# Attention beside a 2-D spectral filter on one core: spent query space reused for exp buffers, longer batches of key steps, and a closing product in three rounded parts

## The chip, the core and the metric

The kernel runs on one core of a Trainium2 chip. The metric is the device time of one execution in microseconds. The kernel before took 642.26 us as the median of three runs (642.26 to 642.81). The engines named below are PE (TensorE; PEld is its loading of weights), DVE (VectorE), ACT (ScalarE), POOL (GpSimd) and SP (SyncE, which here only starts DMAs).

## The reference

Two independent halves, put side by side in the output (2048 x 896):

```python
# half A: B=1, S=2048, D=448, H=16 heads of Dh=28, one key and one value head for all
q = (x @ wq).reshape(B, S, H, Dh).transpose(0, 2, 1, 3)
k, v = x @ wk, x @ wv
p = softmax(einsum("bhqd,bkd->bhqk", q, k) * Dh ** -0.5)
a = einsum("bhqk,bkd->bhqd", p, v).transpose(0, 2, 1, 3).reshape(B, S, H * Dh) @ wo
# half B: x of 2048 x 448, weights of 2048 x 225
y = irfft2(rfft2(x) * (w_r + 1j * w_i))
```

Everything is float32. Where a float32 matmul would be slow, the kernel splits an operand into a rounded high part and a low rest (F32R) and adds the three larger of the four products.

## The kernel before, in words

**The stages.** First come the projections of half A and the first transform of half B. They leave the queries of all heads in `qraw` (128 partitions x 4 groups x 2048 positions, on chip, 1 MB for each quarter of 512 positions), the split keys in `ka` and the values with a column of ones in `vs`. Then follows the main loop, which is nearly the whole time: attention for 4 quarters `c` of the queries times 4 groups `g` of four heads times 16 blocks `kc` of 128 keys, 256 *steps* in that order. A step has, for each of its four heads, a *score* matmul (line 872: 128 keys x 512 queries into one bank of PSUM), an exp of scale times score on ACT into an exp buffer on chip (line 816), and a product with the values (line 827, `flush`), which adds up over the 16 steps in one bank `po`. An exp buffer `p` holds two heads; there are `P_BUFS = 8` of them, so four steps.

**Batches.** Steps are taken in batches, listed in `PLAN`: all scores of a batch are issued first, then the products. `spread` writes out a batch of `n` steps as a string in order of issue: "-" is a score whose exp ACT does straight from PSUM, "k" a score of the batch's last step, which DVE copies to a `k` tile in SBUF (line 878) so that its bank is free early; its exp is done later, in place, two heads in one instruction of ACT (line 895), and the products of this *kept* step come in the next batch (`kept`). "e" is a kept score that ACT exps straight from PSUM. Letters for other work stand among the scores: "A" and "B" are the two matmul units of half B's middle stage (`fft2_a`, `fft2_b`, lines 561 to 563), "Z" its last stage (`fft3_a`, line 660, and `fft3_b`, line 674), "W" a quarter of an output projection of half A (`wo_unit`, line 736), "X" four W, "Y" two Z. `start` and `rest` shift the places. In the list before there are 50 batches: two of one step, four of two, 18 of five and 26 of six.

**What sets the order.** PE, DVE and ACT run in the order of the program. Eight banks of PSUM serve scores, units and the running sum; `take` picks the one that a running estimate (`clock`) has free first and `give` returns it after its last reader. `exps` issues an exp only while fewer than eight buffers are held. DVE's other work (splits of queries in `build_q`, division and split of results in `norm`, splits of weights) waits in `queue` and is put between by `passed` where the estimate has DVE free; `need` forces it. `after(step)` starts what hangs on a step: loads of the next stage (`later`), and at `step % 16 == 3` the split of the next group's queries from `qraw` into `qa`, which eight small DMAs and a large one on SP then spread.

**The end.** After the last batch (lines 907 to 940) the sum of the last group is transposed and divided in four blocks; for each block of 128 queries nine rounded products of the first three groups (`partial`) and one float32 product of the last group with `w3` (`final`, line 918) make the output, which ACT copies (line 741) and sends from its own DMA queue (line 746). A branch follows that is taken only when scores could overflow; it reads `qraw` and isn't taken here.

Of the kernel before, what the change touches and what calls it, by code (L numbers as in the profile page):

```python
# [10 lines left out]
F32 = mybir.dt.float32  # L11
# [12 lines left out]
NG = 4  # L24
NC = 4
# [22 lines left out]
PLAN += [spread(5, "BA", 4, 0.9, 0.6)] + [spread(5, "A")] + 6 * [spread(5, "BA", 4, 0.9, 0.6)]  # L48
PLAN += [spread(5, "BA", 4, 0.75, 0.6)] + 3 * [spread(5, "BA", 4, 0.9, 0.6)] + 2 * [spread(6, "X")]
PLAN += [spread(5, "BA", 4, 0.9, 0.6)] + [spread(6, "BAX")] + [spread(5, "BAB", 4, 0.9, 0.6)]  # L50
PLAN += [spread(6, "BX")] + [spread(6, "Y")] + [spread(5, "")] + 2 * [spread(6, "Y")]
PLAN += [spread(6, "Y", 4, 0.9, 0.6)] + [spread(6, "X")] + [spread(6, "X", 4, 0.9, 0.6)] + [spread(6, "X")]
PLAN += [spread(6, "Y")] + [spread(6, "X", 4, 0.9, 0.6)] + 3 * [spread(6, "Y")]
PLAN += [spread(6, "Y", 4, 0.9, 0.73)] + [spread(6, "Y")] + [spread(6, "Y", 4, 0.9, 0.73)]
PLAN += 3 * [spread(6, "X")] + [spread(6, "Y")] + [spread(6, "X", 4, 0.9, 0.73)] + [spread(5, "Y")]
PLAN += [spread(6, "Y")] + [spread(6, "Y", 4, 1.2)] + [spread(5, "Y")]


WARM = 10, 10
# [3 lines left out]
def kernel(ctx: ExitStack, tc: tile.TileContext, t: dict):  # L63
# [462 lines left out]
    def need(key):  # L526
        while key not in done:
            pop()
# [8 lines left out]
    def at_once(work=640, engine="dve"):  # L537
        clock[engine] = max(clock[engine], clock["pe"] + 200) + work
# [196 lines left out]
                    continue  # L735
                mm(p, x[c][:, g, s], w, start=(g == 0 and n == 0), stop=(g == NG - 1 and n == 2))  # L736

    def wo_out(p, c, k, on_act=False):
        y = pp.tile([128, D], F32, name="yb", tag="p") if on_act else ap.tile([128, D], F32, name="ya")
        if on_act:  # L740
            nc.scalar.activation(y, p, AF.Copy)
        else:
            nc.vector.tensor_copy(y, p)
            at_once()
        r0 = c * CW + k * 128
        (nc.scalar if on_act else nc.sync).dma_start(t["oa"][r0:r0 + 128], y)

    wps = {}

# [17 lines left out]
    def at(step, f, *a):  # L767
        later.setdefault(max(step, 0), []).append((f, a))
# [35 lines left out]
    order = [(c, g) for c in range(NC) for g in range(NG)]  # L804
    kept, po = [], {}

    waiting, held, count = deque(), [0], {}

    def exps():

        while waiting and (waiting[0][2] % 2 or held[0] < P_BUFS):
            sc, tiles, h = waiting.popleft()
            if h % 2 == 0:
                tiles.append(pp.tile([128, 2, CW], F32, name="p"))
                held[0] += 1
            nc.scalar.activation(tiles[-1][:, h % 2], sc, AF.Exp, scale=SCALE)  # L816
            at_once(477, "act")
            give(sc, "act")

    def flush(first, rest=()):  # L820

        for c, g, kc, ps, normal in (*first, *rest):
            n = count[c, g] = count.get((c, g), 0) + 1
            if n == 1:
                po[c, g] = take()
            for i in range(4):
                mm(po[c, g][32 * i:32 * i + 32], vs[:, kc], ps[i // 2][:, i % 2], start=(n == 1), stop=(n == 16))  # L827
            passed(864)
            if n == 16:
                o = osb[c, g] = ap.tile([128, CW], F32, name="osb")  # L830
                nc.vector.transpose(o, po[c, g])  # L831
                at_once()
                if (c, g) != order[-1]:
                    give(po[c, g])
                    norms.append((c, g))
            if normal:
                held[0] -= 2
# [12 lines left out]

    begin = 0
    for tokens in PLAN:
        n = sum(k in "-ke" for k in tokens) // 4
        steps = [(*order[(begin + i) // 16], (begin + i) % 16) for i in range(n)]
        for i in range(n):
            if (begin + i) // 16:
                need(("q", (begin + i) // 16))
        new, lazy, x = [], [], {"-": 0, "k": 0}
        keep = [pp.tile([128, 2, CW], F32, name="k", bufs=4) for _ in range(2)]
        for k in tokens:  # L860
            if k not in "-ke":
                f, *a = todo[k].popleft()
                f(*a)
                continue
            kind = "-" if k == "-" else "k"
            i, h = divmod(x[kind], 4)
            x[kind] += 1
            if kind == "-" and h == 0:
                new.append([])
            c, g, kc = steps[i if kind == "-" else n - 1]  # L870
            sc = take()
            begun.append(mm(sc, ka[:, kc * 128:(kc + 1) * 128], qa[c, g][:, h], start=True, stop=True))  # L872
            passed(232)
            if kind == "-":
                waiting.append((sc, new[i], h))
                exps()
            elif k == "k":
                nc.vector.tensor_copy(keep[h // 2][:, h % 2], sc)  # L878
                at_once()
                give(sc)  # L880
                lazy.append(h)
            else:
                nc.scalar.activation(keep[h // 2][:, h % 2], sc, AF.Exp, scale=SCALE)
# [4 lines left out]
        steps = [(*s, ps, ps is not keep) for s, ps in zip(steps, [*new, keep])]  # L888
        passed(290)
        flush(steps[:1] + kept if n > 4 else kept + steps[:-1], steps[1:-1] if n > 4 else [])  # L890
        kept = steps[-1:]
        clock["act"] += 470 * len(lazy)
        if len(lazy) == 4:
            for p in keep:
                nc.scalar.activation(p, p, AF.Exp, scale=SCALE)  # L895
        else:
            for h in lazy:
                p = keep[h // 2][:, h % 2]
                nc.scalar.activation(p, p, AF.Exp, scale=SCALE)
        after(begin + n - 1)  # L900
        begin += n
    while norms:
# [2 lines left out]
        pop()  # L905

    c = NC - 1
    w3 = ap.tile([128, D], F32, name="w3", tag="ya")
    nc.sync.dma_start(w3, t["wo"][:, NG - 1])
    ws = []  # L910

    def partial(k):
# [1 line left out]
        wo_mm(ws[k], c, k, range(NG - 1))  # L914

    def final(k):
        p = ws[k]
        mm(p, on[:, 128 * k:128 * k + 128], w3, start=False, stop=True)
        wo_out(p, c, k, True)


    flush(kept)
# [1 line left out]
    for k in range(4):  # L924
        divide(c, NG - 1, k)
        s = slice(128 * k, 128 * k + 128)
        nc.vector.transpose(on[:, s], osb[c, NG - 1][:, s])
    for k in (0, 1):
        partial(k)
    for k in (2, 3):  # L930
# [7 lines left out]
    a, b, d = spare  # L938
    rv = nc.values_load(bits.bitcast(I32)[0:1, 0:1])
    with tc.If(rv > int(np.float32(BOUND).view(np.int32))), tc.tile_pool(name="g1", bufs=1) as g1:  # L940
        kf = g1.tile([32, S], F32, name="kf")
        k4 = g1.tile([128, S], F32, name="k4")
        nc.vector.tensor_copy(kf, ka[0:32].bitcast(F32))
# [183 lines left out]
```

## Time and profile before

| | |
|---|---|
| median of 3 runs | 642.26 us (642.26 to 642.81) |
| profiled execution: its time, its span | 642.82 us, 641.0 us |
| granted PE clock | 1.0 |
| busy: PE, ACT, DVE, POOL | 635.7, 550.7, 372.3, 80.1 us |
| first score of the main loop | 70.45 us |
| first score of step 10 (batches of five begin) | 90.21 us |
| first score of step 109 | 304.58 us |
| last product with the values ends | 626.38 us |

How to read it: "busy" counts the time in which at least one instruction of the engine runs. A line in order of time gives the start, the length, the engine, the line of the program, the operation, output<-input, shapes, how many in a row, and in brackets how long the engine was idle before and what ended that. Matmuls overlap: the time that one takes of PE is the distance to the next one's start, not its own length. A float32 matmul stands as two records.

### The profile page before, as it was taken

How to read it: one execution, taken by the hardware profiler on the slowest of the kernel's cores; microseconds unless marked ns; L12 is line 12 of the kernel's file. 1: busy time of each engine (PE TensorE's matmuls, PEld its weight loads, DVE VectorE, ACT ScalarE, POOL GpSimd, SP SyncE). 2: the span in 40 equal slices, each digit the busy share in tenths (PEclk: the TensorE clock that was granted, in tenths of full speed). 3: DMA queues.
4: the chain of work that ended last, by engine and by line, in shares of the span. 5: the costliest groups of instructions: out<-in, count | busy, mean ns of one | idle time of the engine just before them, and what ended most of it. 6: DMA issues, size and time to landing. Idle time of an engine off the chain costs nothing.

```text
span 641.0 us, 12024 instructions
## 1 busy us (share of the span) xinstructions
PE 635.7 (99%) x4470; PEld 381.8 (60%) x4470; DVE 372.3 (58%) x683; ACT 550.7 (86%) x1011; POOL 80.1 (12%) x150
## 2 busy tenths in 40 slices
PE   9999999999999999999999999999999999999997
PEld 6877655556555556655655566556655566556555
DVE  5999628889997934766543523264545332264521
ACT  5554999999999998988899898998999898998981
POOL 3021401011311110000120300003031100200110
PEclk9999999999999999999999999999999999999999
DMA  8755971554835521214241403123241303140001
GB/s 271 268 161 159 262 175 47 143 126 111 205 102 128 142 59 49 79 47 136 63 103 44 115 16 85 39 57 92 55 120 43 88 15 81 44 127 2 30 31 60
DMA packets 36113, 63.83 MB, mean 100 GB/s; under 512 B 7905, under 2 KB 23922, under 8 KB 35084
## 3 DMA queue, kind: packets, MB, share of 16 engines
q1 hardware_dynamic: 30832, 49.60, 28.0%
q0 software_dynamic: 4640, 12.48, 7.8%
q10 hardware_dynamic: 576, 0.92, 0.4%
q8 instruction: 36, 0.59, 0.4%
q14 instruction: 29, 0.24, 0.1%
HBM read 30.04 MB, written 14.75 MB: 70 GB/s over the span
## 4 chain that ended last, share of the span: by engine, by line
PE 98%; DMA 1%; ACT 0%; SPq 0%; issue 0%; ACTq 0%
PE s L872 31%; PE s L827 22%; PE sx L827 9%; PE s L347 6%; PE po L872 5%; PE po L827 4%; PE s L736 4%; PE sx L872 4%; PE s L145 2%; PE s L674 2%; PE s L660 2%; PE pbb L164 1%; DMA raw<-wq 1%; PE s L562 1%; PE s L561 1%; PE s L563 1%
## 5 line engine op out<-in xcount | busy, mean ns | idle before, releaser
L816 ACT ACTIVATE p<-s 128x512 f32<-128x512 f32 x650 | 345.9, 631 | 33.4 <-PE s L872 27.5
L872 PE MATMUL s<-qa,ka 128*128 128x512 f32 x798 | 236.1, 405 | 0.0
L872 PEld LDWEIGHTS s<-qa,ka 128*128 128x128 f32 x798 | 146.7, 188 | 67.7 <-issue 26.8
L878 DVE COPY k<-s 128x512 f32<-128x512 f32 x129 | 82.5, 682 | 106.6 <-PE s L872 106.6
L827 PE MATMUL s<-p,vs 128*32 128x512 f32 x1024 | 121.7, 595 | 0.0
L895 ACT ACTIVATE k<-k 128x1024 f32<-128x1024 f32 x88 | 90.3, 1108 | 0.0
L827 PEld LDWEIGHTS s<-p,vs 128*32 128x32 f32 x1024 | 30.8, 109 | 67.6 <-issue 65.6
L816 ACT ACTIVATE p<-po 128x512 f32<-128x512 f32 x89 | 56.2, 631 | 9.2 <-PE po L872 8.5
L816 ACT ACTIVATE p<-sx 128x512 f32<-128x512 f32 x85 | 53.6, 630 | 3.1 <-PE sx L872 1.9
L827 PE MATMUL sx<-p,vs 128*32 128x512 f32 x416 | 49.3, 594 | 0.0
L872 PE MATMUL po<-qa,ka 128*128 128x512 f32 x120 | 49.2, 410 | 0.0
L872 PE MATMUL sx<-qa,ka 128*128 128x512 f32 x106 | 42.4, 400 | 0.0
L700 POOL DMA_DIRECT2D ol<-ol x36 | 18.1, 510 | 135.9 <-DVE ol L723 69.0
L827 PE MATMUL s<-k,vs 128*32 128x512 f32 x256 | 33.4, 594 | 0.0
L684 POOL TENSOR_TENSOR yo<-y 128x226 f32<-128x226 f32 x16 | 9.5, 596 | 188.0 <-DVE y L680 110.9
L872 PEld LDWEIGHTS po<-qa,ka 128*128 128x128 f32 x120 | 22.5, 188 | 14.6 <-issue 9.2
L827 PEld LDWEIGHTS sx<-p,vs 128*32 128x32 f32 x416 | 12.5, 110 | 27.9 <-issue 27.6
L831 DVE STREAM_TRANSPOSE osb<-s 128x512 f32<-128x512 f32 x10 | 7.2, 715 | 37.0 <-PE s L827 37.0
L878 DVE COPY k<-po 128x512 f32<-128x512 f32 x29 | 19.8, 681 | 14.3 <-PE po L872 14.3
L827 PE MATMUL po<-p,vs 128*32 128x512 f32 x208 | 25.0, 595 | 0.0
L872 PEld LDWEIGHTS sx<-qa,ka 128*128 128x128 f32 x106 | 19.9, 188 | 6.7 <-issue 2.5
L347 PE MATMUL s<-xh,wqh 128*128 128x512 f32 x56 | 23.0, 410 | 0.1
(217 smaller groups left out, 788.1 us busy)
## 6 DMA issues: line engine op xcount, KB each, us to landing
qa<-qa SPq DMA_DIRECT2D x15, 512.0 KB
raw<-xa SPq DMA_DIRECT2D x16, 256.0 KB
xb<-xb SPq DMA_DIRECT2D x8, 512.0 KB
qa<-qh SPq DMA_DIRECT2D x64, 64.0 KB
qa<-ql SPq DMA_DIRECT2D x60, 64.0 KB
ob<-yo SPq DMA_DIRECT2D x16, 226.0 KB
t<-bs SPq DMA_DIRECT2D x16, 225.0 KB
wr<-wr POOLq DMA_DIRECT2D x16, 225.0 KB, 4.2
```

The source lines that it names most:

```text
L145: mm(pa[r0:r0 + 32, e, o0:o0 + n], f[:, 2 * r + k, 2 * p + e, h], cs1[:, 2 * r + k, :n], start=True, stop=True)
L347: mm(pq, w[:, j, gs], x[:, j], start=(j == 0 and n == 0), stop=(j == 3 and n == 1))
L660: mm(pz[:w, j], c2["c", q][:, j, o0:o0 + w], c2["F", q][:, j], start=True, stop=True)
L674: mm(py[:, k], z[:w, r, js], cs3[:w, k], start=True, stop=True)
L684: nc.gpsimd.tensor_tensor(yo[:, 0:2], y1[:, 0], y1[:, 1], op=ALU.add)
L700: nc.gpsimd.dma_start(ol[c][o, g].bitcast(F32), ol[c][r, 0].bitcast(F32))
L736: mm(p, x[c][:, g, s], w, start=(g == 0 and n == 0), stop=(g == NG - 1 and n == 2))
L816: nc.scalar.activation(tiles[-1][:, h % 2], sc, AF.Exp, scale=SCALE)
L827: mm(po[c, g][32 * i:32 * i + 32], vs[:, kc], ps[i // 2][:, i % 2], start=(n == 1), stop=(n == 16))
L872: begun.append(mm(sc, ka[:, kc * 128:(kc + 1) * 128], qa[c, g][:, h], start=True, stop=True))
L878: nc.vector.tensor_copy(keep[h // 2][:, h % 2], sc)
L895: nc.scalar.activation(p, p, AF.Exp, scale=SCALE)
```

## The change

- `spread` can keep **two** steps (`lazy` over 4: eight "k" or "e", `apart` places them). The second kept step's scores lie in two exp buffers; its exps come first after the direct ones, its products at the end of the same batch.
- `PLAN` has 46 batches: two of one step, four of two, 15 of five, 9 of six, 11 of seven and 5 of eight. The batches up to step 109 are as many and as long as before, with some units in other places; from there on it is 21 instead of 25, most with eight kept scores (240 "k" in all instead of 176), and the Z units stand apart instead of in pairs. Steps, units and exps are the same in number.
- Exp buffers are eight named tiles in a deque `spans`. At steps 40, 104 and 168 the quarter's `qraw` goes to a DRAM tensor `qd` (a DMA of 1 MB on SP); three steps later its space joins `spans` as two buffers more, so 10, 12 and 14. The branch that isn't taken loads `qraw` back first.
- The next group's queries are split two steps earlier (`step % 16 == 1`). The loads of half B's last stage wait for another Z (`Z[4q-5] + 1`).
- At the end the last group's result is split too (a copy and a subtraction on DVE a block), and `final` is three rounded products; the load of `w3` goes. The first three outputs leave from SP; the fourth is copied in halves by ACT and DVE and leaves from two queues.

```diff
-def spread(n, units, lazy=4, start=0.9, rest=0.85):
-    m = 4 * n - 4
+def spread(n, units, lazy=4, start=0.9, rest=0.85, apart=1.0):
+    late = 8 if lazy > 4 else 4
+    m = 4 * n - late
     out = [(float(i), "-") for i in range(m)]
-    out += [(j + 0.5 if j < lazy else m + 0.1 * j, "k" if j < lazy else "e") for j in range(4)]
+    out += [(apart * j + 0.5 if j < lazy else m + 0.1 * j, "k" if j < lazy else "e") for j in range(late)]
...
+PLAN += [spread(8, "ZZZ", 8, 0.9, 0.6, 2.0)] + [spread(7, "ZZ", 8, 0.75, 0.72, 2.0)]
+PLAN += [spread(7, "ZZ", 8, 0.6, 0.6, 2.0)] + [spread(8, "ZZZ", 8, 0.6, 0.6, 2.0)]
+PLAN += [spread(6, "X", 8, 0.9, 0.6, 1.5)] + 2 * [spread(6, "X", 8, 0.9, 0.6, 2.0)]
...
+    qd = dp.tile([128, NG, 3 * CW], F32, name="qd")
...
-    pp = pools.enter_context(tc.tile_pool(name="pp", bufs=P_BUFS))
+    pp = pools.enter_context(tc.tile_pool(name="pp", bufs=1))
+    spans = deque(pp.tile([128, 2, CW], F32, name=f"p{i}") for i in range(P_BUFS))
...
-        at(max(where["Z"][4 * q] - 8, where["B"][-1] + 1), fft3_load, q)
+        at(max(where["Z"][4 * q] - 8, where["Z"][4 * q - 5] + 1 if q > 1 else where["B"][-1] + 1), fft3_load, q)
...
-        while waiting and (waiting[0][2] % 2 or held[0] < P_BUFS):
+        while waiting and (waiting[0][2] % 2 or spans):
...
-        if step % 16 == 3 and step < 240:
+        c, g = divmod(step, 64)
+        if c < NC - 1 and g == 40:
+            need(("q", 4 * c + 3))
+            behind(nc.sync.dma_start(qd[:, :, c * CW:(c + 1) * CW], qraw[:, :, c * CW:(c + 1) * CW]), begun[-1])
+        if c < NC - 1 and g == 43:
+            spans.extend(qraw[:, i:i + 2, c * CW:(c + 1) * CW] for i in (0, 2))
+        if step % 16 == 1 and step < 240:
...
+        stay = 1 + (sum(k in "ke" for k in tokens) > 4)
+        keep = [[pp.tile([128, 2, CW], F32, name="k", bufs=4) for _ in range(2)]]
+        if stay > 1:
+            keep.append([spans.popleft() for _ in range(2)])
...
+        flush(normal[:1] + kept if n > 4 else kept + normal, normal[1:] if n > 4 else [])
+        kept = [(*s, ps, False) for s, ps in zip(steps[:-stay - 1:-1], keep)]
+        for i in reversed(range(stay)):
...
+            if i:
+                flush([kept.pop()])
+                spans.extend(keep[i])
+                after(begin + n - 2)
...
-        mm(p, on[:, 128 * k:128 * k + 128], w3, start=False, stop=True)
-        wo_out(p, c, k, True)
+        p, s = ws[k], slice(128 * k, 128 * k + 128)
+        h, l = oh[c][:, NG - 1, s], ol[c][:, NG - 1, s]
+        mm(p, h, woh[:, NG - 1], start=False, stop=False)
+        mm(p, l, wox[:, NG - 2], start=False, stop=False)
+        mm(p, h, wol[:, NG - 1], start=False, stop=True)
+        wo_out(p, c, k, k + 1)
...
+        h = oh[c][:, NG - 1, s]
+        nc.vector.tensor_copy(h, on[:, s])
+        nc.vector.tensor_tensor(ol[c][:, NG - 1, s], on[:, s], h.bitcast(F32), op=ALU.subtract)
```

More of the change, by code (lines that the diff above doesn't have):

```diff
@@ L736, in wo_mm, with wo_out @@
                 mm(p, x[c][:, g, s], w, start=(g == 0 and n == 0), stop=(g == NG - 1 and n == 2))
[L738 to L744, printed above, removed]
-        r0 = c * CW + k * 128
-        (nc.scalar if on_act else nc.sync).dma_start(t["oa"][r0:r0 + 128], y)
+    def wo_out(p, c, k, last=0):
+        y = pp.tile([128, D], F32, name="yb", tag=f"p{k % 2}") if last else ap.tile([128, D], F32, name="ya")
+        r0 = c * CW + k * 128
+        for e in ((0, 1) if last == 4 else (0,)):
+            s = slice(e * D // 2, (e + 1) * D // 2) if last == 4 else slice(0, D)
+            if last and not e:
+                nc.scalar.activation(y[:, s], p[:, s], AF.Copy)
+            else:
+                nc.vector.tensor_copy(y[:, s], p[:, s])
+                at_once()
+            (nc.scalar if last == 4 and not e else nc.sync).dma_start(t["oa"][r0:r0 + 128, s], y[:, s])
     wps = {}
@@ L805 @@
     kept, po = [], {}
-    waiting, held, count = deque(), [0], {}
+    waiting, count = deque(), {}
     def exps():
-        while waiting and (waiting[0][2] % 2 or held[0] < P_BUFS):
+        while waiting and (waiting[0][2] % 2 or spans):
             sc, tiles, h = waiting.popleft()
             if h % 2 == 0:
-                tiles.append(pp.tile([128, 2, CW], F32, name="p"))
-                held[0] += 1
+                tiles.append(spans.popleft())
             nc.scalar.activation(tiles[-1][:, h % 2], sc, AF.Exp, scale=SCALE)
@@ L836, in flush @@
             if normal:
-                held[0] -= 2
+                spans.extend(ps)
                 exps()
@@ L858 @@
         new, lazy, x = [], [], {"-": 0, "k": 0}
-        keep = [pp.tile([128, 2, CW], F32, name="k", bufs=4) for _ in range(2)]
+        stay = 1 + (sum(k in "ke" for k in tokens) > 4)
+        keep = [[pp.tile([128, 2, CW], F32, name="k", bufs=4) for _ in range(2)]]
+        if stay > 1:
+            keep.append([spans.popleft() for _ in range(2)])
         for k in tokens:
@@ L869 @@
                 new.append([])
-            c, g, kc = steps[i if kind == "-" else n - 1]
+            c, g, kc = steps[i if kind == "-" else n - 1 - i]
             sc = take()
@@ L887 @@
                 after(begin + i)
-        steps = [(*s, ps, ps is not keep) for s, ps in zip(steps, [*new, keep])]
+        normal = [(*s, ps, True) for s, ps in zip(steps, new)]
         passed(290)
[L890 to L899, printed above, removed]
+        flush(normal[:1] + kept if n > 4 else kept + normal, normal[1:] if n > 4 else [])
+        kept = [(*s, ps, False) for s, ps in zip(steps[:-stay - 1:-1], keep)]
+        for i in reversed(range(stay)):
+            hs = [h for j, h in lazy if i == j]
+            clock["act"] += 470 * len(hs)
+            if len(hs) == 4:
+                for p in keep[i]:
+                    nc.scalar.activation(p, p, AF.Exp, scale=SCALE)
+            else:
+                for h in hs:
+                    p = keep[i][h // 2][:, h % 2]
+                    nc.scalar.activation(p, p, AF.Exp, scale=SCALE)
+            if i:
+                flush([kept.pop()])
+                spans.extend(keep[i])
+                after(begin + n - 2)
         after(begin + n - 1)
@@ L907 @@
     c = NC - 1
-    w3 = ap.tile([128, D], F32, name="w3", tag="ya")
-    nc.sync.dma_start(w3, t["wo"][:, NG - 1])
     ws = []
```

29 lines of the change are left out of this document (16 added, 13 removed).

## The prediction

> **What bounds the kernel now.** I read the page's busy shares and its chain first, then the instructions in order of time on PE, batch by batch.
>
> ```profile
> span 641.0 us, 12024 instructions
> PE 635.7 (99%) x4470; PEld 381.8 (60%) x4470; DVE 372.3 (58%) x683; ACT 550.7 (86%) x1011; POOL 80.1 (12%) x150
> q1 hardware_dynamic: 30832, 49.60, 28.0%
> PE 98%; DMA 1%; ACT 0%; SPq 0%; issue 0%; ACTq 0%
> ```
>
> The chain is PE from end to end, so only what shortens PE's sequence counts. But a matmul's end is modelled, so "99% busy" hides PE's waits. They come out when the starts are compared. One early batch of five steps with two units:
>
> ```profile
> 153.26 0.50 PE L872 MATMUL po<-qa,ka 128*128 128x512 f32 x1
> 153.60 1.56 PE L872 MATMUL s<-qa,ka 128*128 128x512 f32 x6
> ...
> 155.70 0.37 PE L561 MATMUL s<-ph,g2h 128*128 128x450 f32 x1
> ...
> 156.31 1.10 PE L872 MATMUL s<-qa,ka 128*128 128x512 f32 x4
> ...
> 160.24 1.04 PE L827 MATMUL sx<-k,vs 128*32 128x512 f32 x8
> 161.10 2.76 PE L827 MATMUL sx<-p,vs 128*32 128x512 f32 x24
> 163.79 0.50 PE L872 MATMUL po<-qa,ka 128*128 128x512 f32 x1
> ```
>
> Six scores take 1.56 with 0.40 for the last: (1.56 - 0.40)/5 = 0.2325 us each, 0.93 a step. The probability products of a step take 161.10 - 160.24 = 0.86. An A or B unit takes 156.31 - 155.70 = 0.61. The batch lasts 163.79 - 153.26 = 10.53; less 20 x 0.2325, 5 x 0.86 and 2 x 0.615 there remain **0.35 us that each batch pays for switching** to the products and back (seen as 0.34 instead of 0.23 after the first score). A late batch with Z units and one with W units:
>
> ```profile
> 340.40 0.50 PE L872 MATMUL sx<-qa,ka 128*128 128x512 f32 x1
> ...
> 343.77 1.04 PE L660 MATMUL po<-fi,c 128*113 128x128 f32 x8
> 344.64 1.04 PE L660 MATMUL sx<-fi,c 128*112 128x128 f32 x8
> ...
> 353.29 0.50 PE L872 MATMUL po<-qa,ka 128*128 128x512 f32 x1
> ...
> 379.80 0.50 PE L872 MATMUL po<-qa,ka 128*128 128x512 f32 x1
> ...
> 383.39 0.37 PE L736 MATMUL po<-woh,oh 128*128 128x448 f32 x1
> ...
> 385.62 1.33 PE L872 MATMUL s<-qa,ka 128*128 128x512 f32 x5
> ...
> 393.11 0.73 PE L872 MATMUL s<-qa,ka 128*128 128x512 f32 x2
> ```
>
> A Z unit is 344.64 - 343.77 = 0.87, a group of four W units 385.62 - 383.39 = 2.23. Six steps with two Z: 5.58 + 5.16 + 1.74 + 0.35 = 12.83, measured 12.89. With WWWW: 13.32, measured 13.31. So the price list closes, the switch costs the same with a Z among the scores (a Z costs none of its own), and these batches hardly wait.
>
> Ledger of steps 109 to 255, whose first score starts at 304.58 and whose last product ends at 626.38 (321.8 us): 147 x 0.93 + 148 x 0.86 (one step is carried in) = 264.0; 32 Z = 27.8; 8 WWWW = 17.8; 25 batches x 0.35 = 8.75; sum 318.4. **PE waits there 3.4 us in all**, 0.14 a batch. The same from 90.21 to 304.58 (214.4 us): 99 x 1.79 = 177.2, 32 A or B units 19.7, 4 WWWW 8.9, 19 x 0.35 = 6.65, together 212.4: waits 1.9, of which 0.6 in each of the two batches with an A alone. What the late waits are:
>
> ```profile
> PEld s L872 <- ACT p L816: 6.5, 27, 0.3
> ...
> 458.62 0.50 PE L872 MATMUL po<-qa,ka 128*128 128x512 f32 x1
> ...
> 461.78 0.68 DVE L213 TENSOR_TENSOR ql<-ql,qh 128x512 fp32r<-128x512 f32 x1
> ...
> 463.68 2.64 PE L872 MATMUL s<-qa,ka 128*128 128x512 f32 x9
> ...
> 466.49 1.07 PE L827 MATMUL sx<-p,vs 128*32 128x512 f32 x8
> ...
> 467.64 1.58 ACT L816 ACTIVATE p<-s 128x512 f32<-128x512 f32 x3 [0.39 <-ACT p L816]
> ...
> 615.43 3.53 ACT L816 ACTIVATE p<-s 128x512 f32<-128x512 f32 x7
> ...
> 471.78 0.50 PE L872 MATMUL s<-qa,ka 128*128 128x512 f32 x1
> ...
> 304.60:626.40 321.80, 321.80 (x2121) 187.37 (x2117) 139.39 (x253) 292.92 (x538) 34.82 (x63) 1.00 0.23 62
> ```
>
> Weight loads of scores wait for an exp, that is, for a bank. The batch at 458.62 is the worst (13.16, 0.34 over its list): nine scores after the Z take 2.64 instead of 2.26. ACT turns out an exp every (3.53 - 0.63)/6 = 0.48. At 467.64 it starts again only after the first product has ended (466.49 + 0.86): sixteen exps had filled all eight buffers. ACT is busy 292.9 of 321.8, so it is not the bound, but near it.
>
> **The change, part by part.**
>
> *Fewer batches.* 44 of five or six steps become 40 (all four are saved among the last 147 steps, 25 to 21). 4 x 0.35 = **-1.4 us**. Steps, units and exps stay the same in number. ZZ pairs become single Z's, which by the list above costs nothing.
>
> *Two kept steps, eight scores to DVE.* Late DVE copies go from 100 to 163:
>
> ```profile
> 304.60:626.40 321.80, 62.13 (x100) 1.00 0.23 62
> ...
> L895 ACT ACTIVATE k<-k 128x1024 f32<-128x1024 f32 x50 | 50.8, 1086 | 0.0
> ```
>
> 63 x 0.62 = 39 us more on DVE (0.68 each where they don't overlap: 43), so 139 becomes 180 of about 318, 57%. On ACT an exp of two halves takes 1.02, as much as two of 0.48 plus a start: no change. Banks: seven serve the scores (eight less the sum's). Six steps with two Z now: PE needs 5.58 + 1.74 = 7.3 for its scores, ACT in that time does (7.3 - 0.6)/0.48 = 14 of its 20: six of seven banks are full at the end, hence waits as soon as anything slips. Seven steps with two Z after: 28 x 0.2325 + 1.74 = 8.25; ACT does 16 of 20, DVE its eight copies (5.5) and two results of Z; four banks full. The product of the second kept step comes seventh: 8.25 + 6 x 0.86 = 13.4 against ACT's 0.6 + 20 x 0.48 + 2.04 = 12.2; 1.2 us to spare. So waits should fall. Ends: all 3.4 us gone, or every batch like the worst of now, 21 x 0.34 = 7.1 (+3.7). I take 2.0 left (0.1 a batch, nearer the mean of now than nothing, as other DVE work still falls between copies): **-1.4**. Early batches change in order only: 1.9 to 1.6, **-0.3**; ends -0.7 (all but the A-alone batches) and +0.5.
>
> *Space of the queries.* Three writes of 1.05 MB (128 x 4 x 512 x 4 bytes) at steps 40, 104, 168, on SP. 49.60 MB in 28.0% of 641 us are 276 GB/s: 3.8 us each. Behind them on SP stand the loads of the next stage:
>
> ```profile
> 297.17 1.28 SPq L651 DMA_DIRECT2D c<-t  x2
> ...
> DMA to landing us min/median/max: 3.2/3.4/3.6
> ...
> 307.94 1.91 PE L660 MATMUL s<-fi,c 128*113 128x128 f32 x16
> ```
>
> The load of c issued at 297.2 to 298.5 lands by 302.1; pushed by 3.8 it lands at 305.9, and its first Z comes about 1.2 us earlier than now (after 9 scores instead of 14), at 306.8. Hidden, with 0.9 to spare. The exp that first uses new space runs a batch (10.5) after the write is issued: hidden. The next group's query splits are queued two steps earlier: three DVE operations (0.68 the last, at 461.78) and nine DMAs on SP, moved ahead of what two steps, 4 us, put on DVE and SP; the need() at step 40, seven steps on, finds them done. The loads of c (SP) and fi (POOL) move with the Z's they serve, eight steps ahead as now. All of this is hidden by a batch or more; bare, it is one DVE operation, 0.7, a group. Ends: 0, or three full writes bare, +11.4; I take 0, as DMA has 0.23 share late. Without that cover each write costs what it is late.
>
> *The end.*
>
> ```profile
> 628.05 0.31 DVE L927 STREAM_TRANSPOSE osb<-osb 128x128 f32<-128x128 f32 x1
> ...
> 630.13 0.91 PE L918 MATMUL s<-w,osb 128*128 128x448 f32 x2
> ...
> 631.09 0.36 PE L736 MATMUL s<-woh,ol 128*128 128x448 f32 x1
> ...
> 637.19 0.54 ACT L741 ACTIVATE yb<-s 128x448 f32<-128x448 f32 x1 [0.41 <-PEq L940]
> 637.76 0.34 ACTq L746 DMA_DIRECT2D oa<-yb  x1
> ...
> L678 DVE COPY m<-s 128x226 f32<-128x226 f32 x11 | 4.3, 393 | 7.4 <-PE s L674 7.0
> ```
>
> The full-precision product costs 631.09 - 630.13 - 0.20 = 0.76; three rounded ones 3 x 0.20 = 0.60: four times -0.15 = -0.6. Two more DVE operations per block of 128 columns (0.39 each at most, by L678 with its 226) make the first block ready at 628.36 + 0.78 = 629.1, ahead of its use at 630.13; without that slack they would cost 0.8. The last output is copied in halves on ACT and DVE, 0.39 instead of 0.54: -0.15. The fourth output takes the buffer of the second, whose write leaves 9 x 0.20 + 2 x 0.60 - 0.54 = 2.5 us before; the last write of now has landed at most 641.0 - 637.76 = 3.2 after its issue, so the fourth may wait up to 0.8. Ends 0 and -1.2; I take **-0.7**, as those 3.2 also hold the program's end. The removed load of w3 lies far ahead of its use and gives nothing. The two halves leave from two queues. The Trainium skill (DMA: Bandwidth & Descriptors, "Issuing engines are not separate DMA queues") says that DMAs started from several engines share the same 16 DMA engines and save issue time alone. By it the landing is no earlier, as I have it; were the halves independent, half of 0.83 us (229 KB at 276 GB/s) would go too, and the sum would be -4.2.
>
> **Sum:** -1.4 - 1.4 - 0.3 - 0.7 = -3.8. The profiled execution took 642.82 with its span of 641.0, so it would become 639.0; it lies 0.56 above the median of 642.26, which becomes **638.5**.
>
> **Rivals.** *Waits go altogether* (chance 0.2): -1.4 - 3.4 - 0.7 - 0.8 = -6.3, 636.0. For it: the count of four banks in seven, and exps that stopped at eight buffers. Against: DVE still has work between its copies. The Trainium skill (Perfetto Trace Analysis, "Optimization Strategy") holds that bubbles which repeat can mean that SBUF or PSUM lacks room for the next tile; by that rule this rival would be the likeliest. The trace agrees as to where weight loads wait, but shows the bank, not the buffer.
>
> *The buffers change nothing for PE* (0.17): waits stay 3.4 and 1.9; -1.4 - 0.7 = -2.1, 640.2. For it: ACT's stop at 467.6 costs PE nothing in that batch, as PE is in its products.
>
> *DVE falls behind, slower* (0.14): a copy every third score is every 0.70 us, and DVE needs 0.68, so a split or norm operation among them (0.68 at 461.78, just ahead of the worst batch's waits) holds two banks longer with nothing to catch up. At 0.34 a late batch waits are 7.1: -2.1 + 3.7 = +1.6, 643.9; at 0.5, 647. It decides for slower from 0.32 a batch (3.4 + 2.1 + 1.3 = 6.8 over 21). Against: DVE has 43% free, and the products give it 6 us a batch.
>
> *A late write of the queries* (0.07): a 1 us wait at each of the three, or at the first Z's, makes 641.5.
>
> **How the numbers follow.** Forecast 0.42 (637.3 to 639.8), the rivals 0.2, 0.17, 0.14, 0.07. What a measurement can tell from no change is about 0.2%, 1.3 us: 641.0 to 643.5. Faster 0.42 + 0.2 + 0.17 = 0.79, less 0.03 for a part of the third that slips over; same 0.09; slower 0.15. PE's list without any wait is 642.26 - 1.4 - 5.3 - 0.8 = 634.8, so the range is 634.7 to 641.7; it leaves out the slower cases.
>
> **What would show it.** 40 batches of the list's price from step 10 on; a late batch of seven with two Z at 8 + 6.5 = 14.6 (28 x 0.2325 + 7 x 0.86 + 1.74 + 0.35) when right, 14.9 or more when DVE is late; fewer waits of score loads for exps, or new ones for DVE copies; ACT without its stop at the sixteenth exp; the time from the first W of the end to the last output shorter by 0.7. It is wrong if Z's or products wait for c, for exps of kept steps, or exps for the writes.

## The result, and the profile after

The changed kernel takes **641.07 us** (median of 12 runs) beside 642.60 us of the kernel before on the same chip: ratio 0.9977, 95% interval 0.9969 to 0.9985. That is 0.23% faster, 1.5 us where 3.8 were forecast; it lies in the stated range of 634.7 to 641.7. The main loop gained more than forecast (3.7 us instead of 3.1), and the end, which was to give 0.7, cost 2.6.

The page of the changed kernel, the same parts as were shown of before:

```profile
span 638.6 us, 12210 instructions
PE 630.2 (99%) x4474; PEld 382.9 (60%) x4474; DVE 416.9 (65%) x756; ACT 547.4 (86%) x983; POOL 79.8 (12%) x150
q1 hardware_dynamic: 32848, 53.32, 29.5%
PE 98%; DMA 0%; ACT 0%; DVE 0%; issue 0%; ACTq 0%
```

By this page alone nothing is wrong: PE is still the whole chain and is busy 5.5 us less. Yet the span fell by only 2.4, and more than half of that came before the main loop. Cut at the first score of the main loop and at the end of the last product with the values (all in us, from the trace of each; "waits" are the batches' lengths less the prediction's price list):

| | before | after |
|---|---|---|
| start to the first score | 70.45 | 69.08 |
| main loop | 555.86 | 552.19 |
| waits in it, steps 10 to 108 | 1.91 | 0.97 |
| waits in it, from step 109 on | 3.41 | 2.08 |
| last product to the end of the span | 14.74 | 17.37 |

The end of the last product is set 0.07 us ahead of the 626.38 in the table of the kernel before, alike in every run, so the differences are not touched. The granted PE clock is 1.0 in every stretch of both profiles up to 634 us, so it has no part in them.

**The loop.** A late batch of seven steps with two Z, in order of time on PE:

```profile
588.57 0.50 PE L891 MATMUL sx<-qa,ka 128*128 128x512 f32 x1
...
591.48 1.04 PE L683 MATMUL s<-cs,z 113*128 113x113 f32 x8
...
594.93 1.03 PE L669 MATMUL s<-fi,c 128*113 128x128 f32 x8
...
597.05 1.07 PE L837 MATMUL s<-qraw,vs 128*32 128x512 f32 x8
597.93 1.04 PE L837 MATMUL s<-k,vs 128*32 128x512 f32 x8
...
603.20 0.50 PE L891 MATMUL sx<-qa,ka 128*128 128x512 f32 x1
```

It lasts 603.20 - 588.57 = 14.63; the list gives 14.62. `qraw` as the source of a product is the queries' old space at work as an exp buffer. ACT in that batch:

```profile
589.17 0.60 ACT L826 ACTIVATE qraw<-sx 128x512 f32<-128x512 f32 x1 [0.86 <-PE sx L891]
...
599.03 2.12 ACT L916 ACTIVATE p<-p 128x1024 f32<-128x1024 f32 x2
600.92 2.11 ACT L916 ACTIVATE k<-k 128x1024 f32<-128x1024 f32 x2
603.80 0.60 ACT L826 ACTIVATE qraw<-sx 128x512 f32<-128x512 f32 x1 [0.77 <-PE sx L891]
```

No row between these has a bracket: ACT runs from 589.17 to 603.03 without the stop at the sixteenth exp that the prediction showed in a batch before the change, and goes straight on to the two kept steps. The stretch from step 109 on, whole and for DVE's copies alone (columns as in the prediction: all five engines in the first, DVE in the second), and the waits of weight loads of scores in the late stretch:

```profile
302.30:621.30 319.00, 319.00 (x2120) 188.40 (x2116) 180.50 (x316) 290.14 (x510) 34.34 (x63) 1.00 0.24 65
302.30:621.30 319.00, 107.12 (x163) 1.00 0.24 65
```

```profile
PEld s L891 <- ACT p L826: 2.2, 9, 0.3
PEld s L891 <- ACT qraw L826: 1.2, 5, 0.3
```

DVE is busy 180.5, as forecast, and the waits for exps fell from 6.5 us to 3.4.

**The end.** In order of time, from the last matmuls on:

```profile
626.52 6.74 SPq L757 DMA_DIRECT2D oa<-yb  x4
...
630.95 0.36 PE L944 MATMUL po<-wol,oh 128*128 128x448 f32 x1
632.12 0.36 ACT L753 ACTIVATE yb<-po 128x224 f32<-128x224 f32 x1 [0.78 <-DMA oa<-yb]
632.51 0.38 ACTq L757 DMA_DIRECT2D oa<-yb  x1
632.51 0.39 DVE L755 COPY yb<-po 128x224 f32<-128x224 f32 x1 [5.17 <-ACT yb L753]
```

The fourth output's copy waits 0.78 for a write, and the two halves go one after the other. But DVE's copy ends at 632.90, and the span only at 638.6. What lies between does not count as busy; it stands in the rows of the branch at the end, whose body is passed over. A row gives engine, operation, count, the shortest, median and longest duration in ns, and when the first and the last one started. COMPARE_BRANCH decides on the branch; EVENT_SEMAPHORE waits for or raises a counter by which the engines tell each other that they are done. Before (line 940):

```profile
L940 SPq EVENT_SEMAPHORE  x5: 17/17/17, 626.1 to 633.7; - x5
...
L940 SPq COMPARE_BRANCH  x1: 50/50/50, 623.2 to 623.2; - x1
L940 DVEq COMPARE_BRANCH  x1: 72/72/72, 630.2 to 630.2; - x1
...
L940 DVEq EVENT_SEMAPHORE  x1: 21/21/21, 633.1 to 633.1; - x1
...
L940 ACTq COMPARE_BRANCH  x1: 54/54/54, 638.7 to 638.7; - x1
L940 ACTq EVENT_SEMAPHORE  x1: 17/17/17, 639.2 to 639.2; - x1
```

After (line 969):

```profile
L969 SPq EVENT_SEMAPHORE  x6: 17/17/17, 636.5 to 636.9; - x6
...
L969 PEldq COMPARE_BRANCH  x1: 358/358/358, 628.1 to 628.1; - x1
L969 PEldq EVENT_SEMAPHORE  x1: 51/51/51, 631.4 to 631.4; - x1
L969 DVEq COMPARE_BRANCH  x1: 72/72/72, 633.1 to 633.1; - x1
L969 ACTq COMPARE_BRANCH  x1: 54/54/54, 633.5 to 633.5; - x1
L969 SPq COMPARE_BRANCH  x1: 50/50/50, 633.9 to 633.9; - x1
L969 ACTq EVENT_SEMAPHORE  x1: 17/17/17, 633.9 to 633.9; - x1
L969 DVEq EVENT_SEMAPHORE  x1: 21/21/21, 636.0 to 636.0; - x1
```

ACT, DVE and SP meet the branch when their own work is done, and their next instruction behind the branch's body is the EVENT_SEMAPHORE. From the one to the other ACT takes 0.4 us, DVE 2.9 and SP 2.6 (before: 0.5, 2.9 and 2.9). Before, SP met it at 623.2 and DVE at 630.2, both while PE was still at work, and only ACT met it last. After, SP starts the last write and DVE copies half of the last output, so both meet it at the very end. The landing of the data does not set the end any more: the last part of the last write lands at 639.7 before, 1.3 us ahead of the end of the span, and at 634.6 after, 4.0 us ahead of it.

### The profile page after: what moved, and what is told of

Read it like the earlier page. It is cut to its first block, busy times and chain, and to the rows that moved or that the text cites. A ratio compares the mean times of both kernels' runs of the same rounds, so it can differ in the third digit from the quotient of the medians.

```text
span 638.6 us, 12210 instructions
## 1 busy us (share of the span) xinstructions
PE 630.2 (99%) x4474; PEld 382.9 (60%) x4474; DVE 416.9 (65%) x756; ACT 547.4 (86%) x983; POOL 79.8 (12%) x150
## 4 chain that ended last, share of the span: by engine, by line
PE 98%; DMA 0%; ACT 0%; DVE 0%; issue 0%; ACTq 0%
PE s L891 30%; PE s L837 27%; PE s L355 6%; PE po L891 5%; PE sx L891 5%; PE po L837 4%; PE sx L837 4%; PE s L745 3%; PE s L153 2%; PE s L683 2%; PE s L669 2%; PE po L745 1%; PE sx L745 1%; PE pbb L172 1%; PE s L303 1%; DMA oa<-yb 0%
## 5 line engine op out<-in xcount | busy, mean ns | idle before, releaser
L826 ACT ACTIVATE p<-s 128x512 f32<-128x512 f32 x416 | 227.0, 640 | 22.9 <-PE s L891 20.4
L837 PE MATMUL s<-p,vs 128*32 128x512 f32 x912 | 110.8, 594 | 0.0
L826 ACT ACTIVATE qraw<-s 128x512 f32<-128x512 f32 x150 | 84.3, 635 | 13.3 <-PE s L891 13.1
L916 ACT ACTIVATE k<-k 128x1024 f32<-128x1024 f32 x80 | 83.4, 1141 | 0.0
L891 PE MATMUL sx<-qa,ka 128*128 128x512 f32 x122 | 48.9, 401 | 0.0
L826 ACT ACTIVATE p<-po 128x512 f32<-128x512 f32 x71 | 45.2, 637 | 1.6 <-PE po L891 1.3
L826 ACT ACTIVATE p<-sx 128x512 f32<-128x512 f32 x65 | 41.1, 632 | 4.1 <-PE sx L891 4.1
L837 PE MATMUL s<-qraw,vs 128*32 128x512 f32 x328 | 42.2, 595 | 0.0
L897 DVE COPY p<-s 128x512 f32<-128x512 f32 x41 | 27.3, 685 | 0.7 <-PE s L891 0.6
L916 ACT ACTIVATE p<-p 128x1024 f32<-128x1024 f32 x24 | 24.9, 1134 | 0.0
```

Source lines behind the costliest of these rows:

```text
L897: nc.vector.tensor_copy(keep[i][h // 2][:, h % 2], sc)
```

## The experiments

The theory after this comparison: the loop's gain is the change's own, the end's loss is SP's and DVE's late passing of the branch. Rivals: the loop's gain is chance or comes from the buffers alone; the end's loss is the shared tile, the serial halves or the writes. All runs, in us (before on the same chips 642.4 to 642.6; "loop" is from the first score to the last product, "late waits" are those from step 109 on):

| run | time | ratio to before [95%] | loop | late waits | last product to end |
|---|---|---|---|---|---|
| e1_old_end | 638.58 | 0.9935 [0.9922, 0.9948] | 552.14 | 2.08 | 14.55 |
| e2_new_end | 644.20 | 1.0027 [1.0017, 1.0038] | 555.90 | 3.44 | 16.89 |
| e3_products | 638.01 | 0.9928 [0.9914, 0.9942] | 552.08 | 2.02 | 14.16 |
| e4_no_branch | 636.94 | 0.9913 [0.9900, 0.9926] | 552.10 | 2.04 | 13.83 |
| e5_before_no_branch | 642.33 | 0.9999 [0.9989, 1.0009] | 555.77 | 3.41 | 14.67 |
| e6_before_sp_out | 644.66 | 1.0037 [1.0023, 1.0051] | 555.80 | 3.44 | 16.86 |
| e7_one_kept | 656.84 | 1.0226 [1.0209, 1.0244] | 567.35 | 17.10 | 17.05 |
| e8_space_only | 642.60 | 1.0003 [0.9994, 1.0012] | 556.21 | 3.74 | 14.55 |
| e9_own_tiles | 640.98 | 0.9975 [0.9966, 0.9984] | 552.15 | 2.04 | 17.09 |
| e10_own_halves | 640.58 | 0.9975 [0.9965, 0.9985] | 552.10 | 2.01 | 16.78 |
| e11_act_sends | 639.32 | 0.9956 [0.9942, 0.9969] | 552.19 | 2.07 | 15.64 |

**e1_old_end: the changed kernel with the end of before.**

```diff
...
-        mm(p, h, woh[:, NG - 1], start=False, stop=False)
-        mm(p, l, wox[:, NG - 2], start=False, stop=False)
-        mm(p, h, wol[:, NG - 1], start=False, stop=True)
-        wo_out(p, c, k, k + 1)
+        mm(p, on[:, 128 * k:128 * k + 128], w3, start=False, stop=True)
+        wo_out(p, c, k, True)
...
```

The lines not shown make ACT copy and send all four outputs, from a tile for each, load `w3` again and leave out the split of the last result.

> The changed kernel with the end of the kernel before (one float32 product with w3, four whole outputs copied by ACT and sent from ACT's queue, each with an output tile of its own). Theory (the main loop gave what was forecast and the new end lost it: SP meets the branch late, the fourth output waits for a shared tile, its halves are copied one after the other): 3.4 us under the kernel before, about 639.2, with 14.7 us from the last product of attention to the end of the span, as before. Rival (the end is innocent and the main loop gives less than its profile says): 641.5 or more, as the rounded products then are a gain that is lost.

Measured 638.58: without the new end the change gains 4.1 us. The loss sits in the end, and the loop's gain is the same 3.7 in a second profile.

**e2_new_end: the kernel before with the new end** (tiles for the four outputs not shared).

```diff
...
-        mm(p, on[:, 128 * k:128 * k + 128], w3, start=False, stop=True)
-        wo_out(p, c, k, True)
+        mm(p, h, woh[:, NG - 1], start=False, stop=False)
+        mm(p, l, wox[:, NG - 2], start=False, stop=False)
+        mm(p, h, wol[:, NG - 1], start=False, stop=True)
+        wo_out(p, c, k, k + 1)
...
```

> The kernel before with the new end alone (three rounded products, outputs from SP, the fourth copied in halves by ACT and DVE), but with output tiles that are not shared, so without the wait for the second output's write. Theory: -0.6 for the products, +0.4 for the halves one after the other, +2.5 for SP's late branch: about 2 more than the kernel before, 644.8. As forecast in the prediction: 0.7 less, 641.9.

Measured 644.20: the end alone, on the old loop, makes the kernel slower by 0.27%. It loses 2.15 from the last product on (16.89 against 14.74) though no tile is shared, so the shared tile is not the main part.

**e3_products: only the three rounded products of the new end**; ACT copies and sends all four outputs from tiles of their own.

```diff
...
-            (nc.scalar if last == 4 and not e else nc.sync).dma_start(t["oa"][r0:r0 + 128, s], y[:, s])
+        (nc.scalar if on_act else nc.sync).dma_start(t["oa"][r0:r0 + 128], y)
...
```

> As the one before, but with the three rounded products at the end: of the new end only the products stay, ACT copies and sends all four outputs from tiles of their own, SP starts no DMA there. Theory: 0.6 less than with the old end, about 638.6, and 14.1 us from the last product of attention to the end of the span. Rival (the outputs' landing sets the end whatever the products cost): the same time as with the old end.

Measured 638.01, 0.57 under e1_old_end in the median and 0.39 from the last product on: the products are worth a little less than the 0.6 forecast. The intervals of the two runs overlap, so the size is not sure. This version beats both kernels.

**e4_no_branch: the changed kernel without the fallback for large scores**, that is without the branch, its body and the load of its condition.

```diff
-    rv = nc.values_load(bits.bitcast(I32)[0:1, 0:1])
-    with tc.If(rv > int(np.float32(BOUND).view(np.int32))), tc.tile_pool(name="g1", bufs=1) as g1:
...
```

> The changed kernel without the branch at the end and all that it holds (the fallback for large scores, not taken with these inputs, is left out; nothing else is). Theory (SP and DVE come to the branch only after their last part in the output and the code behind it is fetched then): about 2.6 less than the changed kernel, 638.5, and the span ends some 1.4 us after the last output has landed instead of 4.0. Rival (the time after the landing is the program's closing of semaphores, not the branch): within 0.6 of the changed kernel.

Measured 636.94, 4.1 less than the changed kernel; the stretch after the last product falls from 17.37 to 13.83, by 3.5. The last write now lands 1.1 us ahead of the end instead of 4.0, so the time behind the landing was not the closing of semaphores, as the rival had it. The 3.5 are 0.9 more than SP's 2.6. Part of it is the wait of the fourth output, which is gone although its tile is still shared:

```profile
631.46 0.36 ACT L753 ACTIVATE yb<-po 128x224 f32<-128x224 f32 x1
```

Why it is gone shows in the changed kernel's DMA queues from 629 to 635 us and in its chain (start, length):

```profile
q8 instruction: 1, 0.02, 1.4%
```

```profile
628.94 3.08 DMA oa<-yb
```

One packet of code, of 16 KB, takes 1.4% of 16 engines in 6 us, about 1.4 us. It starts at 629.23, 1.1 us after PE has met the branch at 628.1. The second output's write lands in 16 parts: 15 by 630.87, one only at 632.02, and the fourth output waits for that one. Without the branch no code packet is there, and all 16 land by 630.95. So the branch costs twice. That the late part shared one of the 16 DMA engines with the code is inferred from this; the trace does not name the engine.

**e5_before_no_branch: the kernel before without the same fallback.** The edit is that of e4_no_branch.

> The kernel before without the branch at the end (the fallback left out). Theory (only ACT meets it late there, and its jump is short: 0.4 us from its compare to its next instruction in the trace, beside the landing): 0 to 0.6 less than the kernel before. Rival (the branch costs every kernel the same): as much less as the changed kernel gains by the same cut, about 2.6.

Measured 642.33, no difference: where SP and DVE meet the branch early it costs nothing. So e4's gain is not the price of having a branch but of meeting it late.

**e6_before_sp_out: the kernel before, with SP starting the last four writes** and nothing else changed.

```diff
-        (nc.scalar if on_act else nc.sync).dma_start(t["oa"][r0:r0 + 128], y)
+        nc.sync.dma_start(t["oa"][r0:r0 + 128], y)
```

> The kernel before with its last four outputs started by SP instead of ACT, nothing else. Theory: SP then meets the branch after the last output, so 2.2 to 2.7 us more than the kernel before, about 645. Rival (which engine starts the outputs doesn't matter, the landing does): within 0.4 of the kernel before.

Measured 644.66, slower by 0.37%, and 2.1 us from the last product on. A change of the queue that starts four DMAs gives most of the end's loss by itself. With e5 it shows the cause from both sides.

**e7_one_kept: the changed kernel, its batches as long, but one kept step in each** (`lazy` 4 throughout).

```diff
...
-PLAN += [spread(8, "ZZZ", 8, 0.9, 0.6, 2.0)] + [spread(7, "ZZ", 8, 0.75, 0.72, 2.0)]
+PLAN += [spread(8, "ZZZ", 4, 0.9, 0.6, 2.0)] + [spread(7, "ZZ", 4, 0.75, 0.72, 2.0)]
...
```

> The changed kernel with one kept step in every batch instead of two (the lengths of the batches, the added space and the new end stay). Theory (the second kept step is what keeps the banks from filling: of 28 scores ACT then has 24 and gets through some 16 while PE does the scores and two Z, so eight would be held by seven banks): 0.3 to 0.8 us of waits more in each of the 21 late batches, 647 to 656. Rival (length and buffers carry the gain): within 1 us of the changed kernel.

Measured 656.84, a little above the 647 to 656 expected: the late waits grow from 2.1 to 17.1, 0.7 more in each of the 21 batches. The last scores of its first batch of eight, in order of time on PE:

```profile
312.61 0.72 PE L891 MATMUL s<-qa,ka 128*128 128x512 f32 x2
313.17 0.50 PE L891 MATMUL sx<-qa,ka 128*128 128x512 f32 x1
313.65 0.50 PE L891 MATMUL s<-qa,ka 128*128 128x512 f32 x1
314.12 0.49 PE L891 MATMUL po<-qa,ka 128*128 128x512 f32 x1
```

Scores start every 0.47 to 0.48 us instead of every 0.2325: that is ACT's time for an exp. So every score there waits until an exp has freed a bank. Without the second kept step, batches of seven or eight cost far more than the four switches that they save.

**e8_space_only: the changed kernel with the list of batches and the end of before**; the queries still go to DRAM and their space becomes buffers.

```diff
...
-PLAN += [spread(8, "ZZZ", 8, 0.9, 0.6, 2.0)] + [spread(7, "ZZ", 8, 0.75, 0.72, 2.0)]
...
+PLAN += [spread(6, "BX")] + [spread(6, "Y")] + [spread(5, "")] + 2 * [spread(6, "Y")]
...
```

> The changed kernel with the list of batches and the end of the kernel before: of the change there remain the queries' space as exp buffers (with the writes to DRAM) and the query splits two steps earlier. Theory (the waits of scores are for banks, which buffers alone don't free): within 0.5 us of the kernel before, with late waits near 3.4 by the price list. Rival (exps stopped for want of a buffer, and that kept the banks): about 1.5 less, late waits near 2. A late write would show as waits just after steps 43, 107 and 171.

Measured 642.60, ratio 1.0003: room alone gives nothing (late waits 3.74 against 3.41), and the three writes cost nothing that can be measured. The reverse, the long batches without the added space, was not tried; a batch of eight steps uses up to 14 buffers. So whether the added space is needed as well stays open.

**e9_own_tiles: the changed kernel with four tiles for the last outputs.**

```diff
-        y = pp.tile([128, D], F32, name="yb", tag=f"p{k % 2}") if last else ap.tile([128, D], F32, name="ya")
+        y = pp.tile([128, D], F32, name="yb", tag=f"p{k}") if last else ap.tile([128, D], F32, name="ya")
```

> The changed kernel with a tile of its own for each of the last four outputs (four in place of two). Theory (the fourth output's copy waits 0.78 us for the write of the second, which has the same tile, and all that follows, SP's last issue and its passing of the branch among it, comes later by that): the time from the last product with the values to the end of the span falls from 17.37 us to 16.6, the median by 0.8, to 640.3. Rival (the copy would have waited for the branch's data or something else by then anyway): 17.4 and 641.1.

Measured 640.98, 0.1 less, and 17.09 from the last product on instead of 16.6. A miss. The copy came as early as expected, at 631.53, which is 10.08 after the last product instead of 10.85. But SP got past the branch hardly earlier, at 636.4 instead of 636.5:

```profile
L969 SPq EVENT_SEMAPHORE  x6: 17/17/17, 636.4 to 636.8; - x6
...
L969 SPq COMPARE_BRANCH  x1: 50/50/50, 633.4 to 633.4; - x1
```

SP takes 3.0 here instead of 2.6. In both traces the code packets after the branch begin at 634.16, though SP and DVE meet the branch 0.3 to 0.5 us earlier here; why is open.

**e10_own_halves: in addition a tile for each half of the fourth output.**

```diff
-        y = pp.tile([128, D], F32, name="yb", tag=f"p{k % 2}") if last else ap.tile([128, D], F32, name="ya")
...
+            y = pp.tile([128, D], F32, name="yb", tag=f"p{k + e}") if last else ap.tile([128, D], F32, name="ya")
```

> As the run with four tiles, and the two halves of the fourth output also in tiles of their own, so that DVE needn't come after ACT. Theory (DVE's half came 0.39 us later only because both write one tile): its copy begins with ACT's, the time from the last product to the end falls by 0.4 more, to 16.2, the median to 639.9. Rival (the last matmul is what DVE's half waits for, or both engines can't read the bank at a time): as the run with four tiles alone. The passing of the branch by SP, 2.6 us, stays in either case, so that both stay above 639.

Measured 640.58, with the ratio of e9_own_tiles; 16.78 from the last product on, where 16.2 were expected. The rival holds: DVE still begins when ACT ends, at 631.84.

```profile
631.45 0.36 ACT L753 ACTIVATE yb<-po 128x224 f32<-128x224 f32 x1
...
631.84 0.39 DVE L755 COPY yb<-po 128x224 f32<-128x224 f32 x1 [4.39 <-ACT yb L753]
```

The tile was not what put the halves in series. The bracket shows that DVE's copy waits for a signal of ACT's, so the order lies in the program. Both read one bank; whether that is why the order was set wasn't tried.

**e11_act_sends: as e10, and all five writes started by ACT**, so that SP meets the branch at 616.6 and only DVE meets it late.

```diff
...
-            (nc.scalar if last == 4 and not e else nc.sync).dma_start(t["oa"][r0:r0 + 128, s], y[:, s])
+            (nc.scalar if last else nc.sync).dma_start(t["oa"][r0:r0 + 128, s], y[:, s])
```

> As the run with halves in tiles of their own, but all five writes of the end are started by ACT, so that SP meets the branch early; DVE still copies half of the fourth output and meets the branch late. It parts SP's passing from DVE's. Theory (each of the two needs about 2.6 to 2.9 us to pass, whichever comes last counts): DVE passes at about 1.1 us before its 636.0 of the changed kernel and the end follows 1.7 later, so 15.0 to 15.5 us from the last product to the end and a median of 639.0. Rival (only SP's late passing costs, DVE's lies beside the landing of the last write): 13.9 to 14.3 us, as with ACT copying all four outputs (14.16), and a median of 638.0.

Measured 639.32 and 15.64, near the theory (639.0, 15.0 to 15.5) and far from the rival (638.0, 14.3).

```profile
L969 DVEq COMPARE_BRANCH  x1: 72/72/72, 633.5 to 633.5; - x1
L969 ACTq COMPARE_BRANCH  x1: 54/54/54, 634.2 to 634.2; - x1
L969 ACTq EVENT_SEMAPHORE  x1: 17/17/17, 634.6 to 634.6; - x1
L969 DVEq EVENT_SEMAPHORE  x1: 21/21/21, 636.5 to 636.5; - x1
```

DVE meets the branch 0.7 us before ACT does and is past it 1.9 us after ACT is. Beside e3_products, where DVE has no part in the last copies, its half of the fourth output costs 1.3 us in the median (1.5 from the last product on); SP's part is the 1.1 to 1.5 from 15.64 to the 16.78 of e10 and the 17.09 of e9, although SP, where it starts the writes, lets ACT begin the fourth copy 0.35 earlier (10.08 us after the last product in e10, 10.43 here).

## Why the prediction was right and wrong

*Fewer batches, -1.4.* Right. Batches of seven and eight close on the list with one switch of 0.35 each (14.63 against 14.62 above; the first of eight steps with three Z 17.27 against 17.28), and there are four fewer.

*Late waits, 3.4 to 2.0.* The size is right: measured 2.08, and again 2.01 to 2.08 in six further profiles of the same list. But the reason given for the fall holds for less than half of it, so the size is in part luck. The prediction called the batch at 458.62 the worst, with 0.34. The batch of step 115, five steps with no unit among the scores, is worse; in the trace of before it starts and is followed by the next batch at

```profile
317.45 0.96 PE L872 MATMUL s<-qa,ka 128*128 128x512 f32 x3
...
327.47 0.73 PE L872 MATMUL s<-qa,ka 128*128 128x512 f32 x2
```

It lasts 10.02 against 9.30 by the list, a wait of 0.72. The new list has no batch without units behind step 109, and with that one gone 0.72 of the fall of 1.33 is accounted for. The others wait about as much as before: (3.41 - 0.72)/24 = 0.11 each, and 2.08/21 = 0.10. What the second kept step does is to let batches of seven and eight steps wait no more than those of six did; e7_one_kept takes it away and waits 17.1. Four of 21 batches carry 1.28 of the 2.08, those of seven or eight steps with a whole W group (steps 157, 200, 213, 226).

*Early waits, 1.9 to 1.6.* Undersized: 0.97. All waits beyond the two batches with an A alone (0.54 and 0.60; the others together lie a little under the list) went, which was the far end of this term, -0.7; it came out at -0.94.

*Writes of the queries, 0.* Right: no wait of Z's, products or exps for them, and e8_space_only shows no cost. The 3.8 us for each fit neither of two readings: the first one's data moved in about 2.6 us, at 393 to 426 GB/s in the trace against the mean of 276 used, while from the start of the DMA to its landing the three took 6.7, 6.1 and 4.5 us. Both lie well under the batch of 10.5 us that hid them.

So the loop was forecast at -3.1 and came out at -3.7.

***The end.* "Ends 0 and -1.2; I take -0.7": this step failed.** It is +2.63, outside both ends. By its own terms, from the two traces:
- Products, -0.6: about right. Without the wait the fourth output's copy would begin 10.85 - 0.78 = 10.07 after the last product instead of 10.88, 0.81 earlier. The products give 0.44 of that (10.87 in e1_old_end, 10.43 in e3_products, where ACT still starts the writes). The rest comes because ACT no longer starts the third write between two copies, a gain that the prediction left out.
- The fourth may wait up to 0.8: it waited 0.78, but not for the write's usual length, which would have been over in time, but for the one part that came late beside the code packet. This takes back the 0.81.
- Halves, -0.15: wrong. They ran in series, 632.12 to 632.90 instead of 0.54 in one piece, +0.24.
- What the step left out is the largest: from the start of the last write to the end of the span it took 3.29 us before and 5.71 after. That +2.42 goes to the branch, by e4, e5, e6 and e11. With the -0.03 of the first two points and the +0.24 of the halves it makes the +2.63. The prediction moved three and a half writes to SP and half a copy to DVE and asked only when the data lands. It did not ask what stands behind those instructions on these two engines. The rows were there in the trace of before: DVE's 630.2 to 633.1 beside ACT's 638.7 to 639.2.

Sum by the stretches of the two profiles: -3.7 in the loop, +2.6 at the end, -1.1; the medians say -1.5. The 1.4 us by which the two profiled executions differ before the first score is for the most part not the change: kernels with the new code lie between 69.08 and 70.16 there, those with the old between 69.58 and 70.45. Whether some 0.4 of it is the change's is open.

*The rivals.* Waits did not go altogether, and DVE did not fall behind at 57%. That the buffers change nothing is right of the buffers alone (e8_space_only) and wrong of the change. The Trainium skill (Perfetto Trace Analysis, "Optimization Strategy") takes repeating bubbles as a possible lack of SBUF or PSUM room. Of the two it was PSUM here: SBUF room alone changed the late waits from 3.41 to 3.74, while with the long batches bank room through a second kept step decides between 2.1 and 17.1.

## What to carry to other kernels

Before giving the last piece of work to an idle engine or queue, look at what that engine still has to do after it: branches and closing semaphores are not in its busy time, and here they were free only while another engine was still working. "PE is 98% of the chain" says nothing about the last 15 us, so cut the span at the last event of the loop and make the ledger of the end for itself. And a longer batch pays only with a place for its results: here it needed the second kept step, and the buffers alone gave nothing.

## What the runs showed of the hardware

Getting past the body of this branch took 2.6 to 3.0 us on SP, 2.9 to 3.2 on DVE and 0.4 to 0.5 on ACT, by the time from the compare to the next instruction (on SP in the runs where that instruction had no write to wait for; in e3_products and e11_act_sends it stands 12.6 us behind the compare and the first output lands just ahead of it). On PE the next instruction starts when the last matmul ends (637.0 before, 631.4 after), so its passing can't be read. The Trainium skill (Advanced Engine Details and Errata, "Control Flow Timing") gives about 108 ns for a compare and branch; the compare's own record is of that order (50 to 72 ns on SP, ACT and DVE), but the way behind the body takes some 25 times the 108 ns on SP and DVE. The Trainium skill (Runtime: NRT & Kernel Launch, "Instruction fetch mechanics") says that a taken branch to code outside the window forces a fetch by DMA first. The trace agrees: five packets of the instruction queue, 8 KB each, follow the branch from 633 to 638 us in the changed kernel. In both kernels a packet begins 0.9 to 1.1 us after each compare of SP, DVE, ACT and PE (which packet belongs to which is read from their order), and SP and DVE go on 1.2 to 1.4 us after theirs has ended. ACT goes on before its own begins; why isn't shown.

Such a fetch can also hold up a data write: beside one 16 KB packet a sixteenth of an output's write landed at 632.0 instead of 630.9.
